# First inverse units behind the block's final spectral products, and matrices and weights held for the border to the FFN

## The chip, the cores and the metric

The kernel runs on one core of one Trainium2 chip. The metric is device time of one execution in microseconds (us). Names used below: PE is the matrix engine (TensorE), DVE VectorE, ACT ScalarE, POOL GpSimd, SP the engine whose queue issues most DMAs.

## The reference

```
x = A_u                                       # (1, 2048, 640) f32
sa, ca, ga, sb, cb, gb = (silu(c) @ w_mod) in six rows of 640
h = layernorm(x) * (1 + ca) + sa
K = 2 * Re(sum_n C exp(A dt t))               # S4D kernel per channel, length 2048
y = irfft(rfft(h, 4096) * rfft(K, 4096))[:2048] + h * D_skip
x = x + ga * y
h = layernorm(x) * (1 + cb) + sb
out = x + gb * ((silu(h @ w1) * (h @ w3)) @ w2)    # w1, w3: 640 x 1728, w2: 1728 x 640
```

A long convolution over 2048 tokens for each of 640 channels, done by FFT, and then a gated FFN with 1728 hidden columns. All data are f32.

## The kernel before, in words

**Two halves with a border.** The first half, to about 390 us, is the convolution. Channels go in five blocks of 128 (`NB = 5`). For each block the kernel generates the S4D kernel (POOL, ACT, DVE, PE), transforms it and the tokens (PE, tiles `ps`, `fh`, `fk`), multiplies the spectra (DVE, tiles `fp`) in eight parts `i = 0..7`, and undoes the second transform stage in four pairs `j = 0..3` (PE, tiles `fz`; task `z{b}.{j}.z`). The result is evicted from PSUM (ACT or DVE, tiles `zt`; tasks `z{b}.{j}.v0` and `.v1`) and stored to a scratch tensor in DRAM (`zd<-zt`; tasks `.o0`, `.o1`). At most three `zt` tiles exist, and a new one waits until the store of the third last has landed.

The last step of the inverse transform needs all frequencies of a token, so it reads `zd` back by tokens: `inverse_load` issues four DMAs (`iz<-zd`) and `inverse` multiplies them on PE with the matrices `wd` (tiles `iy`), and DVE adds each result to the token tile `x2[0..3]` (512 tokens each). `wd` holds 16 matrices of 128 x 128 numbers, one for each token residue, 1.05 MB. A *unit* `u = 0..7` is two residues, and each `x2` tile takes two units. Units 0 and 1 (tile `x2[0]`) run before the border for the channels of blocks 0 to 3 (`cut = 512` columns, 256 KB a load); the last 128 columns of `x2[0]` come when block 4 has been stored, through the tiles `izb`. Units 2 to 7 run inside the FFN's first token block, called from `mid`.

The second half is the FFN: four token blocks, each over 14 f-tiles in the order `ORDER = (0, 13, 1, 2, ..., 12)`; tile 13 is the narrow one with 64 columns of `w1` and `w3` each. For each tile, `weights_load` issues three loads (`wr` twice, `w2r` once) of 327,680 bytes each, then splits every weight into a high and a low part: the high part by a cast on ACT (`wh`, `w2h`), the low part by a subtraction on DVE or POOL (`wl`, `w2l`). `up` runs the matmuls into PSUM (tiles `gu`, three banks), `gate` applies the gate (ACT: `th`, `u`, `ah`; DVE: `a`, `al`), and `down` of the tile before accumulates into `acc`. The first two tiles' weights are loaded and split before the border; the first `up` handles both together (45 matmuls, a later tile 30, a `down` 15).

**What sets the order.** Up to the border the order is written by a planner (`Plan.place`): tasks with an engine, a cost, predecessors, ranks and sizes of their DMAs, placed once, and then every engine takes its instructions in this order. Behind the border a scheduler orders the instructions by priorities. In both halves each engine executes strictly in the order of its list, and so does SP with its DMA issues: an issue that waits holds back all that follow.

**The border.** `change` opens the FFN's pools and loads `x2[0]` and `wd`; planner tasks `fw`, `fa`, `fs` load and split the weights of the first two f-tiles; tasks `iz0`, `iz1`, `ir0`, `ir1` are the first two inverse units. Behind the plan come the `izb` loads, eight matmuls without use named `awake0` that keep PE busy, the inverse of the last 128 columns, three more such matmuls, and the layer norm of the first token tile (`ln2`). The last matmul of that inverse is `self.hold`: every DMA that passes through `held_back` waits for it, in the kernel before the loads of `x2[1..3]` and of the inverse units 2 to 7. The FFN's weight loads do not pass through it, and the loads of the third and fourth f-tile stand in SP's queue among the last spectral stores.

Of the kernel before, what the change touches and what calls it, by code (L numbers as in the profile page):

```python
# [10 lines left out]
F32 = mybir.dt.float32  # L11
# [7 lines left out]
P = 128  # L19
# [80 lines left out]
POOLQ = False  # L100
# [71 lines left out]
class Plan:  # L172
# [10 lines left out]
    def add(self, name, eng, took, f, after=(), rank=0.0, port=False, take=(), give=(), table=None, dma=None):  # L183
        assert name not in self.tasks, name
        take = [(r, name + "".join(x), k) for r, k, *x in take]
        if not isinstance(eng, tuple):
            eng, took, f = (eng,), (took,), f and (lambda e, f=f: f())
        self.tasks[name] = (eng, took, f, tuple(after), rank, port, take, tuple(give), table, dma)
# [94 lines left out]
class K:  # L283
# [419 lines left out]
    def weights_load(self, b, m, wp, ahead=False):  # L703

        nc = self.nc
        two = m < 13
        n = 2 if two else 1
        dma = (nc.gpsimd if ahead and POOLQ else nc.sync).dma_start
        raw = wp.tile([P, 2, KT, P], F32, name=f"wr{b}_{m}", tag="wr", bufs=2)
        f0 = m * P  # L710
        for i, src in enumerate((self.w1, self.w3)):
            if two:
                dma(raw[:, i], src[:, f0:f0 + P].rearrange("(k p) f -> p k f", p=P))
            else:
                dma(raw[:, 0, :, i * 64:(i + 1) * 64], src[:, f0:].rearrange("(k p) f -> p k f", p=P))
        w2r = wp.tile([P, D], F32, name=f"w2r{b}_{m}", tag="w2r", bufs=2)
        if two:
            dma(w2r, self.w2[m * P:(m + 1) * P, :])
        else:
            for i in range(2):  # L720
                dma(w2r[i * 64:(i + 1) * 64], self.w2[1664:1728, :])

        parts = []

        def high():
            wh = wp.tile([P, 2, KT, P], F32R, name=f"wh{b}_{m}", tag="wh", bufs=2)[:, :n]
            w2h = wp.tile([P, D], F32R, name=f"w2h{b}_{m}", tag="w2h", bufs=2)
            if b == 3:

                nc.vector.tensor_mul(w2r[:, :512], w2r[:, :512], self.gb)  # L730
            for i in range(n):
                self.nc.scalar.activation(wh[:, i], raw[:, i], AF.Copy)  # L732
            self.nc.scalar.activation(w2h, w2r, AF.Copy)  # L733
            parts.extend((wh, w2h))

        def low(eng):
            wh, w2h = parts
            wl = wp.tile([P, 2, KT, P], F32R, name=f"wl{b}_{m}", tag="wl", bufs=2)[:, :n]
            w2l = wp.tile([P, D], F32R, name=f"w2l{b}_{m}", tag="w2l", bufs=2)
            for i in range(n):  # L740
                eng.tensor_tensor(wl[:, i], raw[:, i], wh[:, i].bitcast(F32), op=ALU.subtract)  # L741
            q = slice(0, P if two else 64)
            if not two:
                self.nc.gpsimd.memset(w2l[64:].bitcast(F32), 0.0)  # L744
            eng.tensor_tensor(w2l[q], w2r[q], w2h[q].bitcast(F32), op=ALU.subtract)  # L745
            return wh, wl, w2h, w2l

        def split():
            high()
            return low(nc.vector)  # L750
        return (high, low) if ahead else split
# [3 lines left out]
    def ffn(self, nxt, wp, pool, ps, po, mid):  # L755

        pend = None
        for b in range(4):
            acc = None
            for i in range(14):  # L760
                m = self.ORDER[i]
                if b == 0 and i < 2:
                    if i == 0:
                        w = [self.ahead.pop((0, x)) for x in range(2)]
                        both = self.up(0, [(self.ORDER[x], *w[x][:2]) for x in range(2)], *nxt[0], ps)
                    w2h, w2l = w[i][2:]
                    gu = both[i]
                else:
                    wh, wl, w2h, w2l = self.ahead.pop((b, i), None) or self.weights(b, m, wp)
                    gu, = self.up(b, [(m, wh, wl)], *nxt[b], ps)  # L770
                if pend is not None:
                    self.down(*pend)
                    if i == 0:
                        self.output(b - 1, pend[1], pool, ps)
                if acc is None:
                    acc = [po.tile([P, 512], F32, name=f"acc{b}{k}", tag=f"acc{k}") for k in range(KT)]
                ah, al = self.gate(b, m, gu, pool)
                pend = (m, acc, ah, al, w2h, w2l)
                mid(b, i)
        real = self.nc  # L780
        nc = self.nc = Engines(self, real)
        self.down(*pend, (4, 0, 1))
        pt = self.turn_last(3, acc, pool, ps)
        self.down(*pend, (2, 3))
        self.output(3, acc, pool, ps, pt)
        self.nc = real
# [71 lines left out]
    def run(self):  # L858
# [7 lines left out]
        def open_(name, side=None, bufs=1, space=None):  # L866
            scopes[name] = ExitStack()
            return self.pool(name, bufs=bufs, space=space, ctx=scopes[name], side=side)

        def close(*names):  # L870
            for n in names:
                scopes.pop(n).close()
# [15 lines left out]
        nc = self.nc = Engines(self, real)  # L888
# [16 lines left out]
        b = NB - 1  # L905

        def change():
            close("gw", "tbl", "gp", "early")
            self.xp, self.ip, self.wp = open_("xp"), open_("ip"), open_("wp")
            self.wd = self.xp.tile([P, NJ, 2, 64], F32, name="wd")  # L910
            self.x2 = [self.xp.tile([P, 4, D], F32, name="x20")]
            nc.sync.behind = nc.tensor.prev
            self.load_x2(0)
            nc.sync.dma_start(self.wd, self.t_wd)
            nc.sync.behind = None
            self.stats = self.ln_begin(self.ip, "n0")
        add = plan.add
        add("change", None, 0, change, [f"g{b}.7.p", f"g{b}.7.d"] + [f"h{b}.{i}.x" for i in range(4)], 0)
        add("fx", "SP", 0, None, ["change"], 0, dma=[327680] * 4 + [1048576])
        self.ahead = {}  # L920
        split = {}
        cut = b * P
        z = {}
        W = self.W["tail"]
# [3 lines left out]
            add(f"fs{m}", "POOL", 5.0, lambda m=m: self.ahead.__setitem__((0, m), split[m][1](self.nc.gpsimd)), [f"fa{m}"], W + 30)  # L928

        def load_w(m):  # L930
            q = nc.gpsimd if POOLQ else nc.sync
            q.behind = nc.tensor.prev
            split[m] = self.weights_load(0, self.ORDER[m], self.wp, True)
            q.behind = None

        def load_z(u):
            z[u] = self.inverse_load(f"iz{u}", self.ip, "iz", 2, 2 * u, 2, 0, cut)

        def first_rows(u):
            self.inverse(2 * u, 2, z[u], psg, "f", 3, 0, cut)  # L940
            for j in (2 * u, 2 * u + 1):
                self.ln_part(self.stats[0], self.x2[0], j, 0, KT - 1)
        for u in range(2):
            add(f"iz{u}", "SP", 0, lambda u=u: load_z(u), ["change", "fx"] + [f"z{b - 1}.{j}.o{f}" for j in range(4) for f in range(2)], W, dma=[262144] * 4)
            add(f"ir{u}", "PE", 2.4, lambda u=u: first_rows(u), [f"iz{u}"] + [f"{x}{b}.{i}.e" for x in ("hh", "k") for i in range(8)], W + 25)
        plan.run()
        self.nc = real
        self.at(1000)
# [1 line left out]
        xp, ip, wp = self.xp, self.ip, self.wp  # L950
        pool = open_("ffn", "right")
        close("psx", "psg")
        po = open_("po", space=PSUM)
        ps = open_("ps", space=PSUM)
        self.x2 += [pool.tile([P, 4, D], F32, name=f"x2{b}") for b in range(1, 4)]
        z = self.inverse_load("izb", ip, "izb", 1, 0, 4, cut, D, real.scalar)
        self.awake(nc.tensor, po.tile([P, 512], F32, name="awake0", tag="acc4"), 8)
        self.hold = nc.tensor.prev = self.inverse(0, 4, z, ps, "gu", 3, cut, D)
        self.awake(nc.tensor, po.tile([P, 512], F32, name="awake1", tag="acc4"), 3)
        nxt = {0: self.ln2(0, pool, ps, self.stats, po)}  # L960
        self.at(2000)
        self.load_x2(1)

        def mid(b, m):
            if b == 0 and m in (1, 3):
                self.load_x2((m + 3) // 2)
            if b == 0 and 2 <= m + 1 < 8:
                self.inverse_unit(m + 1, ip, ps, "gu", 3)
            if b == 0 and m == 9:
                self.gb_row(pool, ps)  # L970
            if m == 8 and b < 3:
                nxt[b + 1] = self.ln2(b + 1, pool, ps)

        self.ffn(nxt, wp, pool, ps, po, mid)
        close("ps", "po", "ffn", "wp", "ip", "xp")

# [584 lines left out]
```

## Time and profile before

| | |
|---|---|
| median of 3 runs | 998.25 us (996.02 to 1000.65) |
| profiled execution, its own time | 998.14 us |
| its span, first to last instruction | 996.4 us |
| mean granted PE clock | 0.975 |
| PE busy | 893.9 us (90%) |
| DVE, ACT, POOL busy | 665.9, 496.8, 287.7 us |
| moved by DMA | 122 MB, 122 GB/s over the span |
| first `up` of the FFN begins | 398.52 us |

How to read the lines shown: one execution, times in us from its first instruction. The chain of waits follows the work that ended last back to what released it. A row of a time line has start, duration, engine, line, operation, output and inputs, count, and in brackets how long the engine had been idle before it and what ended that. `SPq` is SP's queue of DMA issues: such a row's duration is the time that issuing took, waits between the issues included, not the transfer. A row of windows has the stretch, the busy time of each engine with its count of instructions, then granted PE clock, share of the DMA engines' time in use, and GB/s.

### The profile page before, as it was taken

What the parts mean: (1) busy time and instruction counts of PE and PEld (TensorE: products, weight loads), DVE (VectorE), ACT (ScalarE), POOL (GpSimd) and SP (SyncE); (2) the same over time, 40 slices, a digit from 0 to 9 for tenths busy, and PEclk for the clock granted to TensorE, in tenths of its full rate; (3) what the DMA queues carried; (4) which work ended last, traced back from release to release, by engine and by line L of the source; (5) the groups of instructions that cost most, each with busy time, mean ns of one, the idle gap of its engine ahead of it and who ended that gap; (6) DMA issues with size and microseconds to landing.
All of it is one profiled execution on the core that took longest, in us unless ns stands there. A gap on an engine that the chain in (4) does not pass through costs nothing.

```text
span 996.4 us, 20192 instructions
## 1 busy us (share of the span) xinstructions
PE 893.9 (90%) x8095; PEld 708.2 (71%) x8095; DVE 665.9 (67%) x1234; ACT 496.8 (50%) x829; POOL 287.7 (29%) x293
## 2 busy tenths in 40 slices
PE   1464777889999997999999999999999999999997
PEld 1133666767788863667788888888888888888885
DVE  7998999999999674677564553463644544645443
ACT  6878787979788731432243332342432332433221
POOL 1798798989898330100000000000000000000000
PEclk9986998999999999999999999999999999999999
DMA  9955553615041297997232363332443323542301
GB/s 215 266 177 188 123 132 99 156 45 129 24 108 46 73 266 206 221 236 173 61 98 73 106 166 92 86 100 79 118 134 107 92 80 94 145 119 80 106 27 53
DMA packets 141189, 122.03 MB, mean 122 GB/s; under 512 B 13480, under 2 KB 124840, under 8 KB 139688
## 3 DMA queue, kind: packets, MB, share of 16 engines
q1 hardware_dynamic: 140360, 119.84, 45.6%
q8 instruction: 63, 1.03, 0.5%
q10 hardware_dynamic: 736, 0.92, 0.3%
q14 instruction: 30, 0.25, 0.1%
HBM read 99.75 MB, written 20.97 MB: 121 GB/s over the span
## 4 chain that ended last, share of the span: by engine, by line
PE 72%; DVE 13%; DMA 5%; ACT 4%; issue 3%; POOL 1%; SPq 1%; ACTq 0%; DVEq 0%; POOLq 0%
PE acc L833 19%; PE gu L798 13%; PE gu L797 12%; PE gu L796 12%; PE ps L157 4%; DVE yy L157 3%; DMA xs<-in_x 3%; PE kps L157 2%; PE fk L157 2%; PE fz L157 2%; DVE fp L157 2%; DMA zd<-zt 2%; PE fh L157 2%; DVE hn L157 2%; DVE xx L157 2%
## 5 line engine op out<-in xcount | busy, mean ns | idle before, releaser
L798 PE MATMUL gu<-xh,wl 128*128 128x512 f32 x540 | 213.1, 395 | 0.0
L797 PE MATMUL gu<-xl,wh 128*128 128x512 f32 x540 | 211.8, 392 | 0.0
L796 PE MATMUL gu<-xh,wh 128*128 128x512 f32 x540 | 210.7, 392 | 0.7 <-ACT xh L666 0.7
L732 ACT ACTIVATE wh<-wr 128x640 fp32r<-128x640 f32 x105 | 71.9, 732 | 135.6 <-PE gu L797 129.3
L744 POOL MEMSET w2l<- 64x640 f32 x3 | 1.9, 630 | 451.0 <-PE acc L833 451.0
L797 PEld LDWEIGHTS gu<-xl,wh 128*128 128x128 f32 x540 | 101.6, 188 | 23.6 <-DVE xl L667 0.2
L796 PEld LDWEIGHTS gu<-xh,wh 128*128 128x128 f32 x540 | 101.4, 188 | 23.2 <-ACT xh L666 1.0
L798 PEld LDWEIGHTS gu<-xh,wl 128*128 128x128 f32 x540 | 101.6, 188 | 21.3
L809 ACT ACTIVATE th<-gu 128x512 f32<-128x512 f32 x52 | 31.1, 598 | 127.7 <-PE gu L798 127.5
L811 DVE TENSOR_TENSOR a<-a,gu 128x512 f32<-128x512 f32 x52 | 35.8, 688 | 86.2 <-PE gu L798 85.9
L157 POOL TENSOR_TENSOR yy<-e,e 128x512 f32<-128x512 f32 x80 | 86.3, 1094 | 17.9 <-PE kps L157 11.8
L833 PE MATMUL acc<-w2h,ah 128*128 128x512 f32 x220 | 87.1, 396 | 0.0
L833 PE MATMUL acc<-w2l,ah 128*128 128x512 f32 x220 | 87.1, 396 | 0.0
L733 ACT ACTIVATE w2h<-w2r 128x640 fp32r<-128x640 f32 x54 | 39.9, 738 | 94.6 <-issue 53.0
L810 DVE SCALAR_TENSOR_TENSOR a<-th,gu 128x512 f32<-128x512 f32 x52 | 35.7, 687 | 76.1 <-ACT th L809 76.0
L745 DVE TENSOR_TENSOR w2l<-w2r,w2h 128x640 fp32r<-128x640 f32 (+1 forms) x54 | 44.4, 822 | 58.0 <-ACT w2h L733 57.9
L741 DVE TENSOR_TENSOR wl<-wr,wh 128x640 fp32r<-128x640 f32 x105 | 82.4, 819 | 0.0
L157 POOL TENSOR_TENSOR ph<-p,p 128x1024 int32<-128x1024 int32 x40 | 79.9, 1997 | 5.2 <-ACT tr L157 4.5
L833 PE MATMUL acc<-w2h,al 128*128 128x512 f32 x204 | 77.6, 396 | 0.0
L157 DVE TENSOR_TENSOR yy<-yy,tr 128x512 f32<-128x512 f32 (+1 forms) x80 | 75.5, 946 | 0.9 <-ACT tr L157 0.6
L157 PE MATMUL kps<-yy,xx 128*32 128x64 f32 x2560 | 52.7, 239 | 24.9 <-DVE xx L157 21.9
L157 PEld LDWEIGHTS kps<-yy,xx 128*32 128x32 f32 x2560 | 46.1, 119 | 34.5 <-issue 17.5
(231 smaller groups left out, 1694.7 us busy)
## 6 DMA issues: line engine op xcount, KB each, us to landing
wr<-in_w SPq DMA_DIRECT2D x104, 320.0 KB, 3.9
w2r<-in_w SPq DMA_DIRECT2D x52, 320.0 KB, 3.0
zd<-zt SPq DMA_DIRECT2D x39, 256.0 KB, 2.7
iz<-zd SPq DMA_DIRECT2D x24, 320.0 KB, 9.2
xs<-in_x SPq DMA_DIRECT2D x16, 320.0 KB, 11.2
hs<-hb SPq DMA_DIRECT2D x20, 256.0 KB, 2.4
xb<-hs SPq DMA_DIRECT2D x20, 256.0 KB, 4.5
x<-in_x SPq DMA_DIRECT2D x16, 320.0 KB, 9.8
```

The costliest lines, as they stand in the source:

```text
L157: self.prev = self.k.order(f(*a, **kw), self.prev)
L732: self.nc.scalar.activation(wh[:, i], raw[:, i], AF.Copy)
L733: self.nc.scalar.activation(w2h, w2r, AF.Copy)
L741: eng.tensor_tensor(wl[:, i], raw[:, i], wh[:, i].bitcast(F32), op=ALU.subtract)
L745: eng.tensor_tensor(w2l[q], w2r[q], w2h[q].bitcast(F32), op=ALU.subtract)
L796: nc.tensor.matmul(pg, wh[:, k, :], xh[:, k, :], start=(k == 0), stop=False)
L797: nc.tensor.matmul(pg, wh[:, k, :], xl[:, k, :], start=False, stop=False)
L798: nc.tensor.matmul(pg, wl[:, k, :], xh[:, k, :], start=False, stop=(k == KT - 1))
L809: nc.scalar.activation(th, gu[0], AF.Tanh, scale=0.5)
L810: nc.vector.scalar_tensor_tensor(a, th, 1.0, gu[0], op0=ALU.add, op1=ALU.mult)
L811: nc.vector.tensor_mul(a, a, gu[1])
L833: nc.tensor.matmul(acc[k], *two(a, w), start=(m == 0 and i == 0), stop=(m == 12 and i == 2))
```

## The change

- Planner: the loads of units 0 and 1 (`iz{u}`) also wait for the evictions of block 4's pair `u`, and their matmuls (`ir{u}`) for block 4's last inverse matmuls `z4.3.z`. The planner is told two DMAs of 524,288 bytes for each where it had four of 262,144.
- `wd`: only the first four of its 16 matrices are loaded in `change`; the other twelve are loaded behind the hold, after the loads of `x2[1]`.
- Weights: `weights_load` issues each load through `held_back`. The first two tiles' loads come before the hold exists and are as before. The third tile's load is issued ahead of the loads of `x2[1]` (`self.third`) and split inside `ffn`; it and all later ones now wait for the hold.
- `awake0` has three matmuls instead of eight.
- `mid` calls inverse unit `m` at f-tile `m` (2 to 7), where it called unit `m + 1` at f-tile `m` (1 to 6).

```
@@ weights_load
-        dma = (nc.gpsimd if ahead and POOLQ else nc.sync).dma_start
+        def dma(to, src):
+            self.held_back(nc.sync.dma_start(to, src))
@@ ffn
-                    wh, wl, w2h, w2l = self.ahead.pop((b, i), None) or self.weights(b, m, wp)
+                    wh, wl, w2h, w2l = self.third() if (b, i) == (0, 2) else self.weights(b, m, wp)
@@ run, change()
-            nc.sync.dma_start(self.wd, self.t_wd)
+            nc.sync.dma_start(self.wd[:, :4], self.t_wd[:, :4])
...
-        add("fx", "SP", 0, None, ["change"], 0, dma=[327680] * 4 + [1048576])
+        add("fx", "SP", 0, None, ["change"], 0, dma=[327680] * 4 + [262144])
@@ run, load_w()
-            q = nc.gpsimd if POOLQ else nc.sync
+            q = nc.sync
@@ run, units 0 and 1
-            add(f"iz{u}", "SP", 0, lambda u=u: load_z(u), ["change", "fx"] + [f"z{b - 1}.{j}.o{f}" for j in range(4) for f in range(2)], W, dma=[262144] * 4)
-            add(f"ir{u}", "PE", 2.4, lambda u=u: first_rows(u), [f"iz{u}"] + [f"{x}{b}.{i}.e" for x in ("hh", "k") for i in range(8)], W + 25)
+            add(f"iz{u}", "SP", 0, lambda u=u: load_z(u), ["change", "fx"] + [f"z{b - 1}.{j}.o{f}" for j in range(4) for f in range(2)] + [f"z{b}.{u}.v{f}" for f in range(2)], W, dma=[524288] * 2)
+            add(f"ir{u}", "PE", 2.4, lambda u=u: first_rows(u), [f"iz{u}", f"z{b}.3.z"] + [f"{x}{b}.{i}.e" for x in ("hh", "k") for i in range(8)], W + 25)
@@ run, behind the plan
-        self.awake(nc.tensor, po.tile([P, 512], F32, name="awake0", tag="acc4"), 8)
+        self.awake(nc.tensor, po.tile([P, 512], F32, name="awake0", tag="acc4"), 3)
...
         self.at(2000)
+        self.third = self.weights_load(0, self.ORDER[2], wp)
         self.load_x2(1)
+        self.held_back(nc.sync.dma_start(self.wd[:, 4:], self.t_wd[:, 4:]))
@@ run, mid()
-            if b == 0 and 2 <= m + 1 < 8:
-                self.inverse_unit(m + 1, ip, ps, "gu", 3)
+            if b == 0 and 2 <= m < 8:
+                self.inverse_unit(m, ip, ps, "gu", 3)
```

The compiled order of the changed kernel, as far as the prediction speaks of it. SP behind the hold: third tile's weights, `x2[1]`, the rest of `wd`, `x2[2]`, unit 2, fourth tile's weights, `x2[3]`, unit 3, fifth tile's weights. PE in the FFN: the paired `up`, the third tile's `up`, `down` of the first, half of unit 2, `down` of the second, a quarter of unit 2, `down` of the third, around the last quarter of unit 2, the fourth tile's `up`, unit 3. Before, unit 2, the first `down` and the pairs of units and `down` that follow stood between the two `up`. ACT in both kernels: `th` of the first tile, `wh` of the third and fourth tile, gate of the narrow tile, the first `ah`; `wh` of the fifth tile before the third tile's `ah`. `w2h` of the third tile stands before that `ah` in the kernel before and behind it in the changed one.

## Prediction

> **What bounds the kernel now.** I read the page first, then the chain of waits around the border between the convolution and the FFN (340 to 445 us), then the time lines of the DMA queue, ACT and PE there, and last windows of time for granted clock and DMA rate.
>
> ```profile
> PE 72%; DVE 13%; DMA 5%; ACT 4%; issue 3%; POOL 1%; SPq 1%; ACTq 0%; DVEq 0%; POOLq 0%
> ```
> ```profile
> 369.76 8.34 DMA zd<-zt
> ...
> 378.81 5.28 DMA zd<-zt
> ...
> 384.81 3.81 DMA izb<-zd
> ...
> 429.22 3.70 PE acc L833 x15
> ...
> 439.80 1.38 PE iy L652 x8
> ```
>
> The columns of the chain are start, duration, and what it followed. PE carries 72% of it, almost all in the FFN. At the border it does not: from 369.76 to 384.09 the chain follows stores of spectral products (`zd<-zt`), then the last load of the inverse (`izb<-zd`), which lands at 388.62. The store that begins at 378.81 takes 5.28 us. What lies ahead of it in SP's queue, and what comes behind:
>
> ```profile
> 367.48 1.09 SPq L713 DMA_DIRECT2D wr<-in_w  x2
> 368.88 0.43 SPq L718 DMA_DIRECT2D w2r<-in_w  x1
> 369.76 0.37 SPq L157 DMA_DIRECT2D zd<-zt  x1
> 370.83 4.42 SPq L713 DMA_DIRECT2D wr<-in_w  x2
> 375.34 0.84 SPq L718 DMA_DIRECT2D w2r<-in_w  x1
> 376.28 1.64 SPq L157 DMA_DIRECT2D zd<-zt  x2
> ...
> 390.03 3.79 SPq L632 DMA_DIRECT2D x<-in_x  x8
> 393.86 11.31 SPq L642 DMA_DIRECT2D iz<-zd  x8
> 406.16 4.63 SPq L632 DMA_DIRECT2D x<-in_x  x4
> 411.97 10.59 SPq L713 DMA_DIRECT2D wr<-in_w  x4
> ```
> ```profile
> 352.00:358.00 6.00, 6.00 (x82) 4.59 (x79) 5.17 (x10) 2.04 (x4) 0.00 (x0) 1.00 1.05 335
> 374.00:382.00 8.00, 7.66 (x27) 3.09 (x24) 4.63 (x14) 1.79 (x3) 0.00 (x0) 1.00 1.10 334
> 392.00:420.00 28.00, 23.85 (x111) 16.72 (x110) 19.58 (x47) 14.12 (x21) 2.59 (x2) 1.00 1.03 222
> ```
>
> The last three columns of a window are granted clock, DMA share and GB/s. The DMA engines are full on both sides of the border. Ahead of it they carry the weights of the FFN's third and fourth f-tile (the two groups of `wr` and `w2r`) in front of the stores. The first token load at 390.03 marks the hold, the end of the first tokens' inverse; from there the queue carries tokens, the inverse's matrices and, last, the fifth and sixth tile's weights (`wr` x4). The border is bound by DMA; behind it DMA is as full, but PE does not wait for it.
>
> **The change part by part.**
>
> Moved off the border: 0.79 MB of `wd` (three quarters of the 1.05 MB) and six weight loads of 327,680 B, 2.75 MB in all. Where `wd` and the weights are on their way the rate is 334 to 335 GB/s, so 2.75 MB are 8.2 us; at 222 GB/s they would be 12.4. But the engines set a floor:
>
> ```profile
> 365.83 0.75 DVE L157 TENSOR_TENSOR fp<-fp,fk 128x256 f32<-128x256 f32 x2
> ```
> ```profile
> zd<-zt SPq DMA_DIRECT2D x39, 256.0 KB, 2.7
> ```
>
> DVE ends the products of part 6 at 366.6. With the first inverse units out of PE's way part 7 follows at once: an eviction that moves from ACT to DVE (0.7, an estimate from this row, as the next), three product steps (2.1), eight inverse matmuls at the 0.25 us of the row 429.22 (2.0), two evictions (1.4), one store (2.7): 375.5 instead of 384.09, so 8.6 us at most. I take 8.5: the hold falls at 381.5.
>
> Edits with no cost of their own: the two inverse units now stand on PE behind the spectral products, where it has room while the last stores and the `izb` load fly; without that cover they would cost 4 us, at the 1.38 us for eight of the row 439.80 by estimate. The awake matmuls (8 to 3) lie in the same stretch; fewer of them leave PE a pause of about 2 us there. The rest of `wd` is read first by the third inverse unit, far behind the hold. The wait on the hold, added to it and to the weights, stops nothing: the token loads behind it in SP's queue waited on the same hold.
>
> Behind the border: the same 2.75 MB now go into SP's queue after the hold, all of them ahead of the fifth tile's weights. Before, those were the last of 22 loads (x8, x8, x4 and two of the x4): 7.2 MB, at 222 GB/s 32.5 us, and some 2.5 us until the first moves, so 425. ACT's casts agree: the pair from 424.54 to 426.07 ends with one of 0.7 us that began at about 425.3:
>
> ```profile
> 407.80 0.60 ACT L809 ACTIVATE th<-gu 128x512 f32<-128x512 f32 x1 [3.94 <-PE gu L798]
> 408.31 2.62 ACT L732 ACTIVATE wh<-wr 128x640 fp32r<-128x640 f32 x4
> 410.95 0.59 ACT L815 ACTIVATE th<-gu 64x512 f32<-64x512 f32 x1
> 411.45 0.58 ACT L817 ACTIVATE u<-gu 64x512 f32<-64x512 f32 x1
> 412.05 0.63 ACT L666 ACTIVATE ah<-a 128x512 fp32r<-128x512 f32 x1
> ...
> 424.54 1.53 ACT L732 ACTIVATE wh<-wr 128x640 fp32r<-128x640 f32 x2 [3.08 <-PE gu L798]
> 425.97 0.62 ACT L666 ACTIVATE ah<-a 128x512 fp32r<-128x512 f32 x1
> 427.32 0.74 ACT L733 ACTIVATE w2h<-w2r 128x640 fp32r<-128x640 f32 x1 [0.73 <-PE acc L833]
> ```
>
> What the border gains, this train gives back at the same price, so the fifth tile's weights land near 425.3 again, whatever that price is. The question is who waits for them. ACT takes its instructions in order, and in the changed program's list the casts of the fourth tile still stand before the gate of the second (`th` of 64 rows) and the first tile's `ah`, and the casts of the fifth before the third tile's `ah`. Before, the first group (`x4` at 408.31, third and fourth tile) found its weights long landed. Now:
>
> - The fourth tile's weights stand behind 5.7 MB of other loads after the hold. Of these 1.77 MB are weights and `wd` (5.3 us at 335 GB/s) and 3.93 MB tokens and matrices (17.7 at 222); with their own 0.66 MB (2.0) and 2.5 at the start that is 27.5 us, 409. One cast, the gate's two steps and `ah` (0.7 + 0.5 + 0.5 + 0.6, from the starts of the rows above) put the first `down` at about 411.5. PE is free earlier: the first `th` stood 17.8 us after the hold, the paired `up` ends a good 1 us behind it, and the third tile's `up`, which PE's new list puts next, takes 30 matmuls, 6.9 us (from 432.92, the end of the row 429.22, to 439.80): 26.5 us after the hold with its wait for the low halves, 408. It waits some 3 us.
> - Then come 15 matmuls (3.5), twelve inverse matmuls (2.1) and ten matmuls (2.3): at about 419.5 PE stands before the third tile's `down`. That needs the `ah` which on ACT stands behind the fifth tile's casts, and the `w2h` behind that: 425.3 + 0.7 + 0.6 + 0.7 = 427.4. It waits nearly 8 us.
>
> Before, this `down` started at 429.22 (`x15`). It now starts 1.8 us earlier, but with less done: 20 inverse matmuls that had run before are still to come, 3.4 us at the eight in 1.38 of the row 439.80. Net 1.6 us late, and from there on PE is the chain to the end.
>
> The long wait has a second price, the clock:
>
> ```profile
> 71.86 1.98 PE L157 MATMUL ps<-wk,ks 128*64 128x128 f32 x16 [6.78 <-DVE ks L157]
> ...
> 77.13 1.09 PE L157 MATMUL ps<-wk,ks 128*64 128x128 f32 x16
> ```
> ```profile
> 72.00:76.00 4.00, 4.00 (x84) 3.37 (x88) 3.89 (x8) 2.32 (x4) 2.61 (x3) 0.50 0.85 287
> ```
>
> After 6.78 us of idle PE ran 16 matmuls in 1.98 us that take 1.09 a little later, and the granted clock between was 0.50: half rate from 71.86 to nearly 77.13, about 5 us, 2.5 us of work lost. The wait before the third `down` is of that length; what the shorter wait costs in clock is hidden in the longer one. Bounds: 0, and 3.4 if the half rate lasts 7 us. I take 2.5. The Trainium skill, "TensorE: Matmul & The Clock Gate", Part 1, puts the return to full clock at about 3.4 us of sustained work, a loss of 1.7 by estimate; the sum would be 0.8 lower by it.
>
> One more term: where the last stores come later than the moved bytes alone would let them, the train slips by as much: 0 to 3 us, I take 0.4.
>
> Sum: 1.6 + 2.5 + 0.4 = 4.5 us later. The profiled execution took 998.14 us (span 996.4 and 1.7 around it), 0.1 under the median of the runs, 998.25; on the median that gives 1002.7.
>
> **The rivals.**
>
> - *Faster: the train keeps up.* If the loads behind the hold ran at the 334 GB/s seen at 374 to 382, the 9.96 MB up to the fifth tile's weights would be in 30 us after they start, at about 414, before PE asks; then the 8.5 us are kept: 989.8 on the median. The point from which it decides: the weights must land 4.1 us sooner, at 421, which is 266 GB/s over the train; by 425.3 it is 240. Against it: the tokens and matrices make up 6.6 of the 10 MB and ran at 222 with the engines full. For it, in a sentence by itself: the Trainium skill, "DMA: Bandwidth & Descriptors", Specifications, gives a limit of about 358 GB/s per core, well above 222, and no run here shows what holds these loads below it.
> - *Break even: the clock holds.* The waits are as said, but the clock stays at 1.00, or a wait is short enough. A pause of PE without a drop is there, though a shorter one, inside the window 392 to 420 with its clock of 1.00:
>
> ```profile
> 395.38 2.40 PE L691 MATMUL tp<-ident,xn 128*128 128x128 f32 x20 [2.63 <-ACT xn L682]
> ```
>
>   Then +1.6 and the 0.4: 1000.2.
> - *Border gains less.* ACT's new list casts the first tile's weights ahead of the evictions of parts 4 and 5, and waits for those weights. If that holds up DVE's products, the last store lands at 379, DMA idles meanwhile, and the train slips 3.5 us: +7.6, 1005.9.
> - That the change does not do what it says can be left out: the new order stands in the compiled lists of SP, PE and ACT.
>
> **How the numbers follow.** Forecast 0.62, with its own range 1000 to 1005.5; break even 0.15; faster 0.10; less gain 0.13. A measurement of this kernel tells about 0.5%, 5 us, from no change. The forecast's 4.5 lies just under that: I count 0.45 of it as beyond, 0.28, and most of the last rival, 0.12: slower 0.40. Faster by that much is the first rival alone: 0.10. Within: 0.50. The range from 997.5 to 1007 leaves out the faster rival and the far ends of the others.
>
> **What would show it.** Right: the chain before the hold no longer has an 8 us `zd<-zt` piece; SP's first issue behind the hold moves from 390 to about 382; ACT shows long gaps ended by `wr` loads before the fourth and fifth tile's casts; PE has two idle stretches of some 3 and 8 us between 405 and 430 with a granted clock of 0.5 behind the second; the chain there runs through `wr<-in_w`. Wrong: no `wr<-in_w` in the chain after the hold and PE without gaps (faster rival), clock 1.00 throughout (break even), or a hold after 385 (less gain).

## The result: 0.5% slower, and the profile after

The changed kernel takes 1004.13 us (median of 10 runs, 1000.26 to 1006.85), the kernel before 998.25 (10 runs, 996.02 to 1001.06). The ratio is 1.0051, with a 95% interval from 1.0035 to 1.0067: 5.9 us slower, little but clear of the noise. The profiled execution took 1003.67 us, its span is 1001.9.

The chain of waits of the changed kernel, behind the hold (start, duration, what it followed):

```profile
385.52 14.67 DMA x<-in_x
...
400.20 11.59 DMA wr<-in_w
...
415.12 10.31 DMA wr<-in_w
...
428.45 2.50 PE acc L834 x5
```

There is no 8 us piece of `zd<-zt` ahead of the hold any more. Instead the chain now runs through loads behind it, twice through weights. SP's queue of the changed kernel (the duration is that of issuing):

```profile
374.65 1.25 SPq L642 DMA_DIRECT2D izb<-zd  x2
380.60 1.05 SPq L709 DMA_DIRECT2D wr<-in_w  x2
...
398.92 1.68 SPq L709 DMA_DIRECT2D wr<-in_w  x2
...
415.12 13.96 SPq L709 DMA_DIRECT2D wr<-in_w  x6
```

The first issue behind the hold stands at 380.60, where it stood at 390.03. The three rows of `wr` are the third, fourth and, from 415.12, the fifth tile's weights. What ACT does with them:

```profile
409.61 0.74 ACT L733 ACTIVATE wh<-wr 128x640 fp32r<-128x640 f32 x1 [8.58 <-DMA wr<-in_w]
411.81 0.74 ACT L733 ACTIVATE wh<-wr 128x640 fp32r<-128x640 f32 x1 [1.47 <-DMA wr<-in_w]
412.57 0.59 ACT L816 ACTIVATE th<-gu 64x512 f32<-64x512 f32 x1
413.06 0.58 ACT L818 ACTIVATE u<-gu 64x512 f32<-64x512 f32 x1
413.67 0.63 ACT L666 ACTIVATE ah<-a 128x512 fp32r<-128x512 f32 x1
...
425.51 0.74 ACT L733 ACTIVATE wh<-wr 128x640 fp32r<-128x640 f32 x1 [8.38 <-DMA wr<-in_w]
426.51 0.74 ACT L733 ACTIVATE wh<-wr 128x640 fp32r<-128x640 f32 x1 [0.27 <-DMA wr<-in_w]
427.15 0.61 ACT L666 ACTIVATE ah<-a 128x512 fp32r<-128x512 f32 x1
427.67 1.35 ACT L734 ACTIVATE w2h<-w2r 128x640 fp32r<-128x640 f32 x2
```

Two gaps of over 8 us, each ended by a weight load, each with a gate's `ah` behind the cast that waits. PE, with the idle time before the row in brackets, and then two windows (granted clock, DMA share and GB/s are the last three columns):

```profile
414.35 0.79 PE L834 MATMUL acc<-ah,w2h 128*128 128x512 f32 x1 [6.35 <-ACT ah L666]
...
428.45 0.80 PE L834 MATMUL acc<-ah,w2h 128*128 128x512 f32 x1 [4.50 <-ACT w2h L734]
```
```profile
428.00:434.50 6.50, 6.05 (x15) 3.68 (x16) 6.33 (x20) 1.02 (x2) 0.00 (x0) 0.50 0.64 173
434.50:445.00 10.50, 10.50 (x51) 7.66 (x50) 4.13 (x7) 3.11 (x5) 0.00 (x0) 1.00 0.57 145
```

PE stops for 6.35 and 4.50 us, and for the 6.05 us behind the second stop it runs at half clock.

**A common zero.** The first 240 us are the same work in all kernels, but end up to 4 us apart from execution to execution. For single profiles I therefore count from the end of a pause that PE has in every one of them, here in the kernel before and the changed one:

```profile
242.49 1.16 PE L157 MATMUL kps<-yy,xx 128*32 128x64 f32 x64 [1.36 <-DVE xx L157]
```
```profile
241.82 1.16 PE L157 MATMUL kps<-yy,xx 128*32 128x64 f32 x64 [1.36 <-DVE xx L157]
```

From there the hold, the last matmul of the first tokens' inverse, ends after 147.5 us before and 138.7 after, and PE's last matmul after 746.8 and 752.7. The border gained 8.8 us; the FFN gave 14.8 back (599.3 us from the hold to PE's end before, 614.1 after).

The median is of 4 to 10 runs. Each ratio is to the kernel before as it was timed together with that run, where its median lay between 998.25 and 999.43 us.

| kernel | median, us | ratio to before (95%) | to the hold | to PE's end |
|---|---|---|---|---|
| before | 998.25 | | 147.5 | 746.8 |
| changed | 1004.13 | 1.0051 (1.0035 to 1.0067) | 138.7 | 752.7 |
| e1, casts behind gates on ACT | 999.88 | 1.0011 (0.9996 to 1.0025) | 138.5 | 747.0 |
| e1b, the same on ACT and DVE | 992.93 | 0.9946 (0.9921 to 0.9972) | 138.2 | 738.5 |
| e2, fourth tile's weights first | 1003.99 | 1.0038 (1.0020 to 1.0056) | 138.5 | 752.6 |
| e3, nine fillers | 1004.17 | 1.0053 (1.0032 to 1.0073) | 138.2 | 752.3 |
| e3b, four fillers | 1002.47 | 1.0026 (1.0010 to 1.0043) | 138.2 | 751.4 |
| e4, units where they were | 1003.74 | 1.0039 (1.0027 to 1.0052) | 138.4 | 752.3 |
| e5, tokens and units later | 991.29 | 0.9917 (0.9901 to 0.9933) | 138.4 | 738.8 |
| e6, units moved only | 999.80 | 1.0003 (0.9988 to 1.0018) | 146.2 | 746.9 |
| e7, bytes held only | 1007.44 | 1.0079 (1.0058 to 1.0099) | 146.1 | 755.1 |
| e8, tokens by residue | 1028.65 | 1.0300 (1.0282 to 1.0318) | 138.6 | 775.6 |
| e9, e5 and two more awake | 991.98 | 0.9936 (0.9916 to 0.9956) | 138.6 | 738.0 |
| e10, e1b's order in before | 998.62 | 0.9989 (0.9973 to 1.0005) | 146.7 | 745.4 |

### The profile page after: what moved, and what is told of

The parts are those of the page before. It is cut to its first block, busy times and chain, and to the rows that moved or that the text cites. A ratio compares the mean times of both kernels' runs of the same rounds, so it can differ in the third digit from the quotient of the medians.

```text
span 1001.9 us, 20176 instructions
## 1 busy us (share of the span) xinstructions
PE 893.6 (89%) x8085; PEld 709.6 (71%) x8085; DVE 666.3 (67%) x1235; ACT 496.1 (50%) x828; POOL 288.2 (29%) x293
## 4 chain that ended last, share of the span: by engine, by line
PE 71%; DVE 15%; DMA 5%; ACT 3%; issue 3%; POOL 1%; SPq 1%; DVEq 0%; ACTq 0%; POOLq 0%
PE acc L834 19%; PE gu L799 12%; PE gu L798 12%; PE gu L797 12%; PE ps L157 4%; DVE yy L157 3%; PE fz L157 3%; PE fk L157 3%; PE kps L157 2%; DMA wr<-in_w 2%; PE fh L157 2%; DVE fp L157 2%; DVE xx L157 2%; DVE hn L157 2%; DMA x<-in_x 1%
```

## The experiments

I call the loads that SP issues behind the hold, one after the other, the train. Theory: these loads are late, the in-order lists of ACT (and what hangs on it) carry the fourth and fifth tile's lateness to PE, and the half clock adds to it. Rivals: PE has no other work without these weights; the units' later place is at fault; the clock costs nothing; the train could run faster.

**Casts behind the gates (e1, e1b).** Only the order of instructions in ACT's list changes; no wait on another engine is added:

```diff
-                self.nc.scalar.activation(wh[:, i], raw[:, i], AF.Copy)
+                self.after_gate(self.nc.scalar.activation(wh[:, i], raw[:, i], AF.Copy), b, m)
...
+    def after_gate(self, i, b, m):
...
+        g = {2: 13, 3: 1}.get(m) if b == 0 else None
```

> The changed kernel, with one order on ACT altered: in the first token block the casts of the fourth and the fifth tile's weights stand behind the last gate steps of the tiles two before them. DMA is as in the changed kernel. Theory (the loads behind the hold are late, and ACT's order lets this reach PE): the fifth tile's weights still land near 425.4 us, but the first and third down no longer stand behind them; PE goes on where it paused 6.35 and 4.50 us, the clock stays at 1.00 between 400 and 440, and the third down starts near 416 instead of 428.45. Then the border's gain (first up 398.52 to 389.74, 8.8 us) is kept: about 990 us. Rival (PE is simply out of input: weights so late stop PE wherever the casts stand): the waits move to the fourth or fifth tile's up, and the time stays within 3 us of 1004.

It took 999.88 us, 4 less than the changed kernel, not the 14 of the theory. The waits of 6.35 and 4.50 us went, and one of 7.26 came, which another queue carried:

```profile
428.22 1.33 PE L652 MATMUL iy<-iz,wd 128*64 128x320 f32 x4 [7.26 <-DVE x L655]
```

In DVE's list the low halves of the fifth tile's weights stood ahead of the additions that free the inverse unit's PSUM bank. So the same order was put on DVE (`wl` behind the gate and the additions of the unit before) and the cast of `w2` (`w2h`) behind the gate of the tile before:

> As the first experiment, but with the same order on DVE too: the fourth and fifth tile's low halves behind the gate and behind the additions of the inverse unit before, and the fifth tile's second cast behind the fourth tile's gate. Loads as in the changed kernel. In the first experiment PE's pause of 7.26 us at 420.95 was ended by DVE's addition of an inverse result, which stood behind the low halves of the fifth tile. Theory (in-order queues carry the late landing to PE, ACT's and DVE's alike): the fifth tile's weights land near 425 us again, but no PE pause over 1 us follows the first up and the clock stays at 1.00; 990 to 991. Rival (PE has no more work without these weights): a pause of 5 us or more stays, now before the fifth tile's up, and the time is 998 or more.

ACT and PE of this kernel, and a window of it:

```profile
427.96 0.74 ACT L737 ACTIVATE wh<-wr 128x640 fp32r<-128x640 f32 x1 [10.18 <-DMA wr<-in_w]
```
```profile
432.16 2.09 PE L652 MATMUL iy<-iz,wd 128*64 128x320 f32 x12 [1.05 <-DVE a L818]
```
```profile
398.00:445.00 47.00, 45.79 (x201) 32.74 (x201) 28.47 (x72) 15.61 (x25) 0.00 (x0) 1.00 1.07 238
```

The fifth tile's cast still waits for its load, until 427.96 (182.4 from the zero; 183.7 in the changed kernel). But PE has one pause of 1.05 us, clock 1.00, and the time is 992.93: the loads were late, and PE had other work all along. From the hold to PE's end it takes 600.3 us, so 13.8 of the 14.8 us that the FFN had lost are back; they hang on the place of a few casts and subtractions in two lists. The median is 2 us above the 990 to 991 that I expected; the seven runs lie between 989.05 and 997.80. The same order in the kernel before:

> The kernel before with the orders on ACT and DVE that took the waits out of the changed kernel, and nothing else. Theory: before the change no cast of a later tile stood late in front of a gate, PE has no pause over 1 us behind the first up, so the order brings nothing: 998 to 999. Rival (the order is worth something by itself): 994 or less, and part of what that experiment gained has nothing to do with the change.

998.62, no gain clear of the noise. The order is worth something only where the loads are late, as the theory says.

**The first wait taken away (e2).** The fourth tile's weights are loaded right behind the third's:

```diff
         self.third = self.weights_load(0, self.ORDER[2], wp)
+        self.fourth = self.weights_load(0, self.ORDER[3], wp)
```

> The changed kernel, with the fourth tile's weights loaded right behind the third's, ahead of all tokens; the bytes ahead of the fifth tile's weights are the same. Theory (only the last wait counts): the pause of 6.35 us before the first down vanishes, PE is at the third down near 416 and waits there some 12 us for the same landing near 425.4; the time stays at 1004 within 2 us. Rival (each wait costs by itself): 6 us faster, near 998.

```profile
414.36 1.26 PE L652 MATMUL iy<-iz,wd 128*64 128x320 f32 x6 [1.68 <-DMA iz<-zd]
428.88 0.79 PE L834 MATMUL acc<-ah,w2h 128*128 128x512 f32 x1 [10.06 <-ACT w2h L734]
```

Of the first wait 1.68 us are left, the second grew to 10.06, and the time is 1003.99: a wait ahead of a later and longer one costs nothing.

**The clock (e3, e3b).** Matmuls by zeros fill the second wait:

```diff
+        for _ in range(9):
+            f = self.nc.tensor.matmul(acc[4], self.zero, v, start=False, stop=False)
```

> The changed kernel, with nine matmuls by a matrix of zeros (they add nothing) between the second and the third down, 0.47 us each, where PE paused 4.50 us; the third down now stands whole ahead of the fourth tile's up. Theory (the pause costs 3.0 us of clock besides the wait): the granted clock stays at 1.00 from 428 to 434, the third down starts at the same time within 0.5 us, and the time is 3 us lower, 1001. Rival (the half clock is not brought on by the pause, or costs nothing since what follows waits anyway): 1004, and with the fillers in the way more.

```profile
423.67 7.89 PE L1526 MATMUL acc<-wd,zero 128*128 128x512 f32 x18
```

The third `down` also stands whole ahead of the fourth tile's `up` here. The time did not fall: 1004.17. My size was wrong: such a matmul has two records (x18 for nine) and takes 0.88 us. The fillers ended 3 us too late, and the third `down` began at 432.71. But PE's end was not later: counted from the zero the third `down` began 3.2 us later than in the changed kernel, with four more inverse records done (0.6), and PE ended 0.5 us earlier. 3.2 - 0.6 + 0.5 = 3.1 us were saved, with the clock at 1.00 from 419.15 on; half of 6.05 is 3.0.

> As the experiment with nine fillers, with four: nine took 7.89 us (0.88 each, not 0.47) and pushed the third down to 432.71, 4.26 us behind the changed kernel's, yet the last matmul ended only 0.6 us later. With four, 3.5 us, they end before the third down's weights are ready. Theory (the pause costs about 3.0 us of clock beside the wait): clock 1.00 from 424 to 440, third down at 428.5 to 429.5, and 3 us below the changed kernel: 1001. Rival (the clock costs nothing): 1004.

```profile
423.62 3.60 PE L1526 MATMUL acc<-wd,zero 128*128 128x512 f32 x8
427.15 0.76 PE L652 MATMUL iy<-iz,wd 128*64 128x320 f32 x4
431.27 1.07 PE L652 MATMUL iy<-iz,wd 128*64 128x320 f32 x4 [3.36 <-DVE x L655]
```

Four fillers left a pause of 3.36 us, on DVE's additions as in e1, and half clock from 431.58 to 434.99, 1.7 us of loss instead of 3.0; the time is 1002.47, 1.7 less than the changed kernel, where I expected 3. The intervals of the two ratios overlap, so this gain is not clear of the noise; from the zero PE ends 1.3 us sooner. That the clock costs is supported; neither run isolates its price, since both moved other work too.

**The order of the train (e5, e9).** The loads of tokens and of the inverse units (`iz`) wait behind the weights that are needed sooner, and the units run three f-tiles later:

```diff
-            if b == 0 and m in (1, 3):
-                self.load_x2((m + 3) // 2)
-            if b == 0 and 2 <= m < 8:
-                self.inverse_unit(m, ip, ps, "gu", 3)
+            if b == 0 and m in (3, 5, 7):
+                self.load_x2((m - 1) // 2)
+            if b == 0 and 5 <= m < 11:
+                self.inverse_unit(m - 3, ip, ps, "gu", 3)
```

Besides, `x2[1]` is no longer loaded right behind the hold, and each token or `iz` load is ordered behind the last weight load issued before it in the program.

> The changed kernel, with the loads behind the hold in another order: third and fourth tile's weights and the rest of the matrices, first token tile, fifth and sixth tile's weights, and only then the other tokens and the inverse matrices, whose units run three f-tiles later. Work and bytes are the same. Theory (train order is what costs): no PE pause over 1 us behind the first up (389.7), clock 1.00 there, weights of the fifth tile before 412; the time is 998.25 less the 8.8 us of the border: 989 to 990. Rival (the units' later place on PE, not the loads, is what made the changed kernel slow): units still later cost still more, 1005 to 1010.

SP's queue and the stretch behind the first `up`:

```profile
385.02 0.95 SPq L710 DMA_DIRECT2D wr<-in_w  x2
...
404.57 0.96 SPq L710 DMA_DIRECT2D wr<-in_w  x2
...
419.02 1.82 SPq L632 DMA_DIRECT2D x<-in_x  x4
```
```profile
389.00:445.00 56.00, 55.77 (x239) 44.89 (x238) 27.41 (x37) 22.68 (x35) 2.59 (x2) 0.97 0.77 187
```

The fifth tile's weights are issued at 404.57, PE is busy for 55.77 of 56 us, and the time is 991.29, 0.83% under the kernel before (ratio 0.9917, 0.9901 to 0.9933). Like e1b (0.9946) it beats both kernels, but by another way: here the loads come in time. The clock of e5 in that window is 0.97, half from 388.89 to 392.30, behind a pause of 2.59 us. Two more awake matmuls were to close that pause:

> The experiment with late units, with five awake matmuls behind the hold instead of three. There PE paused 2.59 us before the layer norm's transposes (385.25 to 387.84) and the granted clock was 0.50 from 388.89 to 392.30. Theory (the pause brings on the half clock, 3.41 us of it, 1.7 us of work): pause under 1 us, clock 1.00 there, and 1.7 us below the 991.3 of the kernel with late units: 989.6. Rival (that window comes whatever PE does, or the matmuls delay the transposes): no gain, or 1 us slower.

```profile
387.07 2.40 PE L692 MATMUL tp<-ident,xn 128*128 128x128 f32 x20 [0.87 <-ACT xn L683]
```

The pause shrank to 0.87, the clock stayed at 1.00, and from the zero PE ended 0.8 us sooner, half of what I expected. The median, 991.98 against 991.29, does not show it: as a gain in time it is not confirmed.

**The train's rate (e8).** Token loads cut by residue, into 128 partitions:

```diff
-            for q in range(4):
-                ...dma_start(self.x2[b][q * 32:(q + 1) * 32], self.xv[q, :, 4 * b:4 * b + 4, :])
+            for j in range(4):
+                ...dma_start(self.x2[b][:, j], self.xv[:, :, 4 * b + j, :])
```

> The changed kernel, with the token loads behind the hold (x2[1..3], 3.93 MB) cut by token residue, each into 128 partitions, instead of by 32 partitions; bytes, number and place of the loads are the same. Theory of the prediction's first rival (the train need not run at 222 GB/s: these loads go to few partitions, and the weights, which go to 128, ran at 287 to 346 in their stretches): a token load lands every 1.0 to 1.1 us instead of 1.5, the fifth tile's weights land 4 to 5 us sooner, and the time falls by 4 to 7 us, to 997 to 1000. Rival (the engines are full whatever the shape): 1.5 us each, 1004.

Both missed: the token loads landed 3.2 us apart at first and up to 6.4 us where other loads shared the way, and the time is 1028.65. PE, and a window in which tokens make up nearly all that moves (320 KB in 3.24 us are 101 GB/s):

```profile
431.66 0.80 PE L838 MATMUL acc<-ah,w2h 128*128 128x512 f32 x1 [21.84 <-ACT ah L670]
455.07 0.80 PE L838 MATMUL acc<-ah,w2h 128*128 128x512 f32 x1 [13.65 <-ACT w2h L738]
```
```profile
397.00:405.00 8.00, 7.88 (x34) 5.88 (x33) 2.81 (x4) 1.90 (x4) 0.00 (x0) 1.00 0.26 102
```

The DMA engines are in use for 0.26 of their time there; in the changed kernel it is 1.00 over the whole train (window further below). As a test of a faster train it failed, but it is one of a slower train: the same two waits, 21.84 and 13.65 us, third `down` at 455.07, and 24.5 us more in time, close to the 23.8 by which that `down` came later from the zero. The landing of the late loads sets the time.

**The two halves of the border (e6, e7).** First the units moved without the bytes, then the bytes without the units.

```diff
-            nc.sync.dma_start(self.wd[:, :4], self.t_wd[:, :4])
+            nc.sync.dma_start(self.wd, self.t_wd)
...
-            self.held_back(nc.sync.dma_start(to, src))
+            nc.sync.dma_start(to, src)
```

> The changed kernel without its two moves of bytes: all of the inverse matrices are loaded before the border and the FFN's weight loads do not wait for the hold; the first inverse units stay behind the spectral products, units 2 to 7 one f-tile later, three awake matmuls. Times are taken from the end of PE's pause near 241 us, which all kernels have; to the first issue behind the hold the kernel before takes 147.5, the changed one 138.8. Theory (the 2.75 MB set the border): 147 to 148 again. Behind it 6.6 MB stand before the fifth tile's weights as in the kernel before; they land 34 us after the hold, the third down waits 3 to 4 us for them with 20 inverse matmuls less done: 1001 to 1003. Rival (the units out of PE's way make the border's gain): 143 to 144 to the hold, and 994 to 998.

```diff
-... + [f"z{b}.{u}.v{f}" for f in range(2)], W, dma=[524288] * 2)
+..., W, dma=[262144] * 4)
...
-            add(f"ir{u}", "PE", 2.4, lambda u=u: first_rows(u), [f"iz{u}", f"z{b}.3.z"] + ...
+            add(f"ir{u}", "PE", 2.4, lambda u=u: first_rows(u), [f"iz{u}"] + ...
```

> The other half: weights and three quarters of the inverse matrices wait for the hold, but the first inverse units stand where they stood before, units 2 to 7 at the f-tile where they were, eight awake matmuls. Theory (the units have to be out of PE's way for the 2.75 MB to count in full): 142 to 143 us from the pause near 241 to the hold, 4 behind the changed kernel; the fifth tile's weights land 45 us after the hold with 16 more inverse matmuls done: 1004 to 1006. Rival (they never stood in the way, PE has room there): 139 to the hold, 1001 to 1002.

Each half alone brings the hold only to 146.2 and 146.1, where both together bring 138.7. With the units moved only, the chain still runs through the last stores; with the bytes held only, it runs through the units and then through the eight `awake0` matmuls (two records each):

```profile
379.33 5.18 DMA zd<-zt
...
384.54 3.22 DMA izb<-zd
```
```profile
360.04 7.90 DMA iz<-zd
...
368.07 1.92 PE iy L157 x6
...
370.71 1.55 DVE st_n L157 x8
...
374.96 1.43 DVE st_n L157 x7
...
378.19 2.30 PE fz L157 x8
...
381.21 7.13 PE awake L157 x16
```

DMA is nearly full in the one and half idle in the other (376 to 388, last but one column: 0.88 with the units moved, 0.49 with the bytes held):

```profile
376.00:388.00 12.00, 6.24 (x17) 1.95 (x16) 5.33 (x20) 0.00 (x0) 0.00 (x0) 0.97 0.88 229
```
```profile
376.00:388.00 12.00, 9.95 (x29) 4.16 (x25) 2.94 (x8) 1.68 (x3) 0.00 (x0) 1.00 0.49 132
```

With the bytes held and the units in place, PE's last spectral matmuls end 136.3 us from the zero, in the changed kernel 128.8: the units cost 7.5 us there, with their wait for `iz` and DVE's additions and statistics ahead of the last products, where I had written 4. The eight `awake0` matmuls, which this run has where the changed kernel has three, are not what holds it up: the last `izb` load landed at 388.92, 1.4 us ahead of the hold, as in the kernel before (1.4) and the changed one (1.5), so they end about when PE gets its data anyway. Both theories of that run missed its hold, and at 1007.44 it is the slowest but one: the train starts 7 us later than in the changed kernel and is as long. PE pauses in it for 6.4 us (for `iz` alone) and not for 10.9, and its end comes 2.4 us later. With the units moved only PE pauses 1.79 us instead of 3 to 4, and the time is that of the kernel before.

**The units' place in the FFN (e4).**

```diff
-            if b == 0 and 2 <= m < 8:
-                self.inverse_unit(m, ip, ps, "gu", 3)
+            if b == 0 and 2 <= m + 1 < 8:
+                self.inverse_unit(m + 1, ip, ps, "gu", 3)
```

> The changed kernel with units 2 to 7 at the f-tile where they were before, one earlier. The fifth tile's weights have the same bytes in front of them, the fourth's 1.31 MB more. Theory (the landing of the fifth tile's weights sets the time): it stays near 425, PE pauses longer before the first down (about 10 us) and has 16 more inverse matmuls behind it at the third, 2.65 us: 1001.5. Rival (the units' later place is what made the kernel slow): back at the border's full gain, 990 to 994.

```profile
406.81 1.30 PE L652 MATMUL iy<-iz,wd 128*64 128x320 f32 x2 [5.89 <-DMA iz<-zd]
...
416.68 0.79 PE L834 MATMUL acc<-ah,w2h 128*128 128x512 f32 x1 [3.96 <-ACT ah L666]
```

1003.74. The rival is out: the units' later place is not what costs. My own number missed too: in this order PE waits 5.89 us for `iz` and 3.96 for the fourth tile's cast, ahead of the third tile's `up`, and not for the fifth tile at all. It waits for other loads of the same train and pauses about as long (11.1 us with a third pause of 1.2, against 10.9).

## Why the prediction was right

The prediction said 1002.7 us, 4.5 more than before; it is 1004.13, 5.9 more. By its steps:

- *The border, 8.5 us earlier:* 8.8. The size is right, the sentence "the border is bound by DMA" only half so: a chain of PE and DVE through the first inverse units was only 1.4 us shorter than the DMA's, and the change removed both. The 8.2 us for the bytes were worth 1.4 as long as the units stood in the way (e7), and the 4 us for the units without their cover were too little: 7.5.
- *The train gives back what the border gains:* the fifth tile's weights at 425.3; their casts began at 425.51 and 426.51. The train from 380.60 on holds 9.96 MB up to here, and its last two loads were in when the second of these casts began: 217 GB/s from the first issue on, 229 if the 2.5 us that I had set aside for the start are left out, as in my 240 (the window shown below has 231, with what moved meanwhile of the loads behind). Counted from the zero, the last load landed 1.9 us later than I had said (184.7 instead of 182.8).
- *The waits, 3 and 8 us:* 6.35 and 4.50. The fourth tile's weights came later than my 409: ACT's second cast waited for them until 411.81. This error had no price, since the wait moved from the second place to the first (e2).
- *Third `down` at 427.4:* 428.45, counted from the zero 0.1 us sooner than before, not 1.8. The 20 inverse matmuls still to come were there (84 instead of 64 records behind it), at 0.15 each 3.0 us instead of 3.4. Net 2.9 instead of 1.6 and 0.4.
- *The clock, 2.5 us:* half clock for 6.05 us of work, 3.0. The 1.7 that I had estimated from the Trainium skill, "TensorE: Matmul & The Clock Gate", Part 1 (about 3.4 us of sustained work), is too low for this trace.
- *Sum:* -0.1 + 3.0 + 3.0 = 5.9 against the 6.0 from the zero and 5.9 in the medians. The two mis-sized terms are the train's rate, which put the third `down` 1.7 us later than I had said, and the clock, 0.5 too low. The inverse matmuls were 0.4 too high, and the 0.4 for a train that slips was not needed: the hold came 0.3 us sooner from the zero than I had said. Together these make the 1.4 by which the sum fell short.

The first rival (a train that keeps up at 334 GB/s, or at the 266 from which it decides) has the DMA engines in use all the time in its way, at 231 GB/s:

```profile
380.60:426.50 45.90, 34.18 (x138) 24.56 (x138) 18.85 (x43) 14.80 (x22) 2.59 (x2) 0.89 1.00 231
```

The second (the clock holds) is ruled out by the 0.50, the third (less gain at the border) by the hold. What the prediction did not see is how little held the loss in place: it named ACT's order as the way by which the landing reaches PE, but not that this order is nearly the whole loss, 13.8 of 14.8 us (e1b).

## What to carry to other kernels

Bytes moved off one border queue up at the next: ask not whether they land before they are used, but which instruction first waits for them and what stands behind that one in its engine's list, for every engine that touches them. Where two chains end at the same place within a microsecond or two, taking one away alone gives next to nothing (1.3 and 1.4 us here), and an experiment on each half alone would have condemned a change whose halves together give 8.8 us. And of several waits in a row for loads of one queue, only the last counted here: what removed an earlier one (e2) moved nothing, since the later load landed no sooner.

## What the runs showed of the hardware

**The clock looks at fixed windows.** In all traces the granted clock changes in steps of 3.41 us. Behind 200 us and up to the last 20 us, in the 14 traces, a step was at 0.50 after a step at 1.00 in which PE had been idle for 1.80 us or more (33 cases), and stayed at 1.00 where it had been idle for up to 1.93 (about 3100 cases); it went back to 1.00 after a step at 0.50 with at most 0.56 us of idle time (33 cases) and stayed at half from 0.54 on (25). So a pause of 2.6 us costs or not by how it lies in the steps: the pause of 2.6 to 2.7 us ahead of the transposes was followed by half clock in the changed kernel, e2, e5, e6 and e7, and by none in eight others. And the step in which PE starts again does not count if 0.6 us of it are idle: half clock then lasts one step more, which is why 6.05 us of work ran at half clock behind the second stop and not 3.4. The Trainium skill, "TensorE: Matmul & The Clock Gate", Part 1, tells of a free-running activity window of this length, and the trace agrees.

**A token load into 128 partitions ran on few DMA engines.** In e8 each such load raised its semaphore 5 times, where the token loads of the other kernels and the weights and `iz` loads raise theirs 16 times; the loads landed 3.2 us or more apart instead of 1.5, and with tokens on their way the engines were in use for 0.26 of their time, about 4 of 16. The Trainium skill, "DMA: Bandwidth & Descriptors", "Why a DMA increments its semaphore by 16 and not by 1", lets the outermost dimensions of both sides decide: here the source's outermost has 4 entries, so 4 engines and one write of the sequencer, as the trace has it.
